# A planner that follows events, two engines that share a rate, later ranks for three pairs, and decay products ahead of the transpose

## The chip, the cores and the metric

The kernel runs on one core of a Trainium2 chip. Five engines take part: TensorE (PE: matrix products; PEld is its loading of weights), VectorE (DVE), ScalarE (ACT), GpSimd (POOL) and SyncE (SP), which here only issues transfers. Each engine works off its own list of instructions in a fixed order and waits on semaphores where it needs another's result. The metric is the device time of one execution in microseconds; a lower one is better.

## What is computed

Three layers follow each other. The first is a linear attention with a decaying state, for 4 batches, 8 heads, 768 steps and head dimension 48:

```
for t in range(S):
    cur     = einsum('bhd,bhe->bhde', u * k[t], v[t])
    y[t]    = einsum('bhd,bhde->bhe', r[t], state + cur)
    state   = w[t][..., None] * state + einsum('bhd,bhe->bhde', k[t], v[t])
```

Its output, as 3072 tokens of 384 values, goes through two gated layers (all in float32):

```
x = (sigmoid(x @ w_gate) * (x @ w_val)) @ w_out        # 384 -> 1536 -> 384
h = x @ w_in                                           # 384 -> 2048
out = (h * tanh(softplus(h))) @ w_out2                 # 2048 -> 384
```

## The kernel before

**Stages.** The 768 steps are cut into 24 chunks of 32 steps, taken two at a time: 12 pairs. For each pair the recurrence is brought into matrix form. `fine(p)` multiplies r and k within blocks of 1, 2 and 4 steps into tiles pt (L515, the helper `times`; GpSimd, for pair 0 also VectorE, by the tuple `SHARED`), sums them over the head dimension into the tile A (L535, VectorE), multiplies the diagonal by u (L515 on VectorE), and after each level folds decays into r, k and w in place (L515, blk). After three levels w at every eighth step holds the decay of eight steps.

`coarse(p)` turns r, k and w to head-dimension-first with VectorE's 32x32 transposes (`flip_k` L633 into KD, `flip_r` L629 into RD, `flip_w` L640 into WD), multiplies parts of RD by decays in WD (`scaled`, L652, three calls, on GpSimd or VectorE), and makes the score products on TensorE (`scores`, L669), whose result `merge` (L690) copies into X beside the turned A (L679). In `flip_w` the four decays of eight steps are turned, and then two small products (L644) make those of sixteen and of 32 steps. `keys(p)` folds the later decays into k, for which a small GpSimd product (`join`) first makes the decay of the last sixteen steps in place, turns k (L723, into KT) and lets ScalarE gather it into KK (L738). `states` and `states_apart` multiply keys and values on TensorE (L795, L841) and add them to the decayed state (`decay`, L772; L824, L852). `rows_out(p)` multiplies X with v and RD with the state (L887), splits the result into a high and a low half-precision part xs (L915, L918), and `turn` brings it to xt, token-last: for pairs 0 and 1 on TensorE (L939), later with a transposing transfer.

The first gated layer works on pairs of 256 tokens. `gate(p, i)` makes 24 groups of nine products per pair (L1011; twelve blocks f, each with a group for the gate and one for the value), three for each of three 128-deep parts, since every operand is held as a high and a low half. ScalarE applies the sigmoid (L1022), VectorE the product (L1027), and both split the result into gt (L1039, L1042). `out1` multiplies gt with the output weights (L1079). The weights come as 64-bit words and are decoded once on the core: `decode` and `decode_early` rescale on ScalarE (L275, L265), join on VectorE (L319, L414), cast the high part on ScalarE (L330, L424) and subtract it for the low part on GpSimd or VectorE (L333, L427). The second gated layer works on six blocks of 512 tokens (L1189, L1304) after the whole attention has ended.

**What sets the order.** The program first collects tasks. Each has one or several engines with a cost in microseconds, the tiles that it reads and writes, and a rank, its place in the program. `Plan.run` walks back from the end and gives every task a due time (`late`) from the costs and waits behind it; TensorE's tasks are due in the order of their ranks, so a rank that comes later means a later due time for all that leads to it. Then it deals out the tasks: for each engine the moment at which it could begin something that is ready, among what is ready there the earliest due; the engine with the earliest moment is served first. A task with two engines goes to the one that is served. The order found is then emitted, once and for all; the costs do not depend on what other engines do.

The main loop runs over pairs p and, in it, over the gate's twelve blocks f. Before block `YPOS[0]` = 4 it places the tasks of `tail1(p + 1)` (coarse, keys, the first states and rows of the next pair), before block `YPOS[1]` = 7 those of `tail2(p + 1)` and of `fine(p + 2)`, with the loads of pair p + 3 and of later values. SyncE's queue issues those loads in the planned order.

## Time and profile before

| | us |
|---|---|
| three runs | 939.11, 939.24, 943.17 |
| median | 939.24 |
| the profiled execution | 943.15 |
| its span | 941.4 |

The profile is of that one execution. The span runs from its first instruction to its last; 1.75 us of the execution lie around it. Busy times are sums of an engine's instructions. The row of an instruction or a group names the line of the kernel, the engine, the operation, the tile written and the tiles read, and shapes as partitions x elements; where a helper issues the instruction, the line is the helper's, so that L515 stands for products of several stages. Groups of the order of time can merge neighbours of one line under the shape of the first.

### The profile page before, as it was taken

What the parts mean: (1) busy time and instruction counts of PE and PEld (TensorE: products, weight loads), DVE (VectorE), ACT (ScalarE), POOL (GpSimd) and SP (SyncE); (2) the same over time, 40 slices, a digit from 0 to 9 for tenths busy, and PEclk for the clock granted to TensorE, in tenths of its full rate; (3) what the DMA queues carried; (4) which work ended last, traced back from release to release, by engine and by line L of the source; (5) the groups of instructions that cost most, each with busy time, mean ns of one, the idle gap of its engine ahead of it and who ended that gap; (6) DMA issues with size and microseconds to landing.
All of it is one profiled execution on the core that took longest, in us unless ns stands there. A gap on an engine that the chain in (4) does not pass through costs nothing.

```text
span 941.4 us, 29364 instructions
## 1 busy us (share of the span) xinstructions
PE 867.8 (92%) x12808; PEld 700.7 (74%) x12808; DVE 652.7 (69%) x1122; ACT 496.2 (53%) x1140; POOL 491.7 (52%) x543
## 2 busy tenths in 40 slices
PE   0376789999999999999999979999999999999998
PEld 0265678888888888888888866667677676776788
DVE  7999986487766768676779886675655556555541
ACT  2677876252525345252539656675555655556540
POOL 7997931556384655647462463553443434434330
PEclk9997979999999999999999999999999999999999
DMA  9164762222222322322216910010200102000000
GB/s 340 64 229 151 252 157 89 78 58 84 75 67 70 98 68 81 91 69 67 54 44 163 281 40 12 13 40 1 69 1 18 52 2 68 2 18 18 1 35 35
DMA packets 55313, 74.26 MB, mean 79 GB/s; under 512 B 19600, under 2 KB 36496, under 8 KB 55056
## 3 DMA queue, kind: packets, MB, share of 16 engines
q1 hardware_dynamic: 55184, 72.38, 25.6%
q8 instruction: 100, 1.64, 0.7%
q14 instruction: 29, 0.24, 0.1%
HBM read 58.99 MB, written 9.44 MB: 73 GB/s over the span
## 4 chain that ended last, share of the span: by engine, by line
PE 78%; DVE 10%; POOL 5%; ACT 4%; issue 2%; DMA 1%; SPq 0%; DVEq 0%; ACTq 0%; POOLq 0%
PE gv L1011 23%; PE h L1189 20%; PE o L1304 18%; PE o L1079 12%; PE yp L887 3%; POOL blk L515 2%; ACT KK L738 1%; PE kp L795 1%; POOL pt L515 1%; PE lp L669 1%; DVE RD L652 1%; DVE word_wp L319 1%; DVE wps L359 1%; DVE word_wi L319 1%; POOL wos L333 1%
## 5 line engine op out<-in xcount | busy, mean ns | idle before, releaser
L1189 PE MATMUL h<-x,wis 128*128 128x512 f16 x864 | 199.9, 379 | 0.0
L1011 PE MATMUL gv<-xt,wgs 128*128 128x256 f16 x1296 | 169.3, 277 | 12.7 <-DVE gt L1042 10.4
L1223 POOL TENSOR_TENSOR sum<-e 128x256 f32<-128x256 f32 x96 | 71.4, 743 | 190.8 <-ACT e L1200 190.8
L1079 PE MATMUL o<-gt,wos 128*128 128x256 f16 x1296 | 165.5, 274 | 3.1 <-POOL wos L333 1.6
L1011 PE MATMUL gv<-xt,wvs 128*128 128x256 f16 x1296 | 166.1, 276 | 1.7 <-ACT sig L1022 1.7
L1011 PEld LDWEIGHTS <-wgs 128*128 128x128 f16 x1296 | 126.3, 99 | 31.5 <-DVE gt L1042 10.7
L1189 PEld LDWEIGHTS <-wis 128*128 128x128 f16 x864 | 83.5, 98 | 82.9
L1079 PEld LDWEIGHTS <-wos 128*128 128x128 f16 x1296 | 126.5, 98 | 21.6 <-issue 1.9
L1011 PEld LDWEIGHTS <-wvs 128*128 128x128 f16 x1296 | 127.1, 99 | 18.7 <-issue 1.9
L515 POOL TENSOR_TENSOR blk<-blk 128x384 f32<-128x384 f32 (+1 forms) x138 | 120.8, 894 | 28.2 <-DMA blk<-rkw 21.0
L515 POOL TENSOR_TENSOR pt<-blk 128x384 f32<-128x384 f32 x93 | 105.0, 1156 | 27.6 <-DMA blk<-rkw 24.3
L1200 ACT ACTIVATE e<-h 128x512 f32<-128x512 f32 x96 | 57.5, 599 | 86.9 <-PE h L1189 85.9
L1027 DVE SCALAR_TENSOR_TENSOR gv<-gv,sig 128x512 f32<-128x512 f32 x72 | 50.6, 702 | 59.2 <-PE gv L1011 24.1
L1022 ACT ACTIVATE sig<-gv 128x512 f32<-128x512 f32 x72 | 42.1, 596 | 91.3 <-PE gv L1011 91.0
L1039 ACT CAST gt<-gv 128x512 f16<-128x512 f32 x72 | 42.1, 585 | 74.3 <-DVE gv L1027 74.2
L772 POOL TENSOR_TENSOR s<-s,WD 128x384 f32<-128x384 f32 x42 | 35.9, 864 | 75.9 <-DVE s L824 44.8
L1304 PE MATMUL o<-wps,gt 128*128 128x192 f16 x612 | 74.0, 246 | 0.0
L738 ACT COPY KK<-KT 32x192 f32<-32x192 f32 (+1 forms) x176 | 64.3, 365 | 5.4 <-DVE KT L723 2.8
L1242 DVE SCALAR_TENSOR_TENSOR gt<-e,gt 128x256 f16<-128x256 f32 x41 | 27.5, 681 | 49.6 <-ACT gt L1237 49.6
L1042 DVE TENSOR_TENSOR gt<-gv,gt 128x512 f16<-128x512 f32 x72 | 49.4, 687 | 16.9 <-ACT gt L1039 16.3
L1304 PE MATMUL o<-wps,wgs 128*128 128x192 f16 x498 | 59.4, 246 | 0.0
L1304 PE MATMUL o<-wps,wos 128*128 128x192 f16 x456 | 57.1, 246 | 0.0
(112 smaller groups left out, 1466.9 us busy)
## 6 DMA issues: line engine op xcount, KB each, us to landing
v<-vt SPq DMA_DIRECT2D x24, 480.0 KB, 4.1
blk<-rkw SPq DMA_DIRECT2D x22, 384.0 KB, 3.5
raw_wi<-wi SPq DMA_DIRECT2D x8, 768.0 KB, 5.3
raw_wp<-wo SPq DMA_DIRECT2D x8, 768.0 KB, 5.8
blk<-rkw SPq DMA_DIRECT2D x11, 512.0 KB, 4.1
raw_wg<-wg SPq DMA_DIRECT2D x6, 768.0 KB, 6.3
raw_wv<-wv SPq DMA_DIRECT2D x6, 768.0 KB, 5.0
raw_wo<-wo SPq DMA_DIRECT2D x6, 768.0 KB, 5.9
```

Of the source, the lines that this page charges most:

```text
L515: engines[e].tensor_tensor(out=pv, in0=a, in1=b, op=ALU.mult)
L738: nc.scalar.copy(out=to, in_=own)
L1011: nc.tensor.matmul(gps[p, i, o][:, h], w[:, a, kc, fs], xt[p][:, c, kc, :], start=(n == 0), stop=(n == 3 * KC - 1),)
L1022: nc.scalar.activation(out=sgs[p, i], in_=gps[p, i, 0], func=AF.Sigmoid, scale=1.0 / (SW * SX))
L1027: nc.vector.scalar_tensor_tensor(out=gps[p, i, 1], in0=gps[p, i, 1], scalar=SG / (SW * SX), in1=sgs.pop((p, i)), op0=ALU.mult, op1=ALU.mult,)
L1039: nc.scalar.copy(out=gt[p][:, 0, 2 * i : 2 * i + 2], in_=gps[p, i, 1])
L1042: nc.vector.tensor_tensor(out=gt[p][:, 1, 2 * i : 2 * i + 2], in0=gps[p, i, 1], in1=gt[p][:, 0, 2 * i : 2 * i + 2], op=ALU.subtract,)
L1079: nc.tensor.matmul(ops[p, c][:, :NT], wos[:, a, f, cs], gt[p][:, g, f, :], start=(f == 0 and n == 0), stop=(f == NF1 - 1 and n == 2),)
L1189: nc.tensor.matmul(hps[r, f], w2["wi"][:, a, kc, fs], x2[r][:, c, kc, :], start=(n == 0), stop=(n == 3 * KC - 1),)
L1200: nc.scalar.activation(out=es[r, f], in_=hps[r, f], func=AF.Mish, scale=ih)
L1223: engines[e].tensor_tensor(out=sums[0][:, n - 1], in0=a(), in1=b(), op=op)
L1304: nc.tensor.matmul(ops2[h, first], home(slots[r, i, name])[:, c, tsl], w2["wp"][:, a, w, i, :], start=(new and n == 0), stop=(n == 3 * NF2 ...
```

## The change

The planner's second half is replaced by a simulation that steps from event to event. A task that reads or writes the port shared by VectorE and GpSimd carries a mark `port`: all tasks that GpSimd may do, and VectorE's whole joins and the product with u. While both engines are at marked tasks, VectorE's proceeds at 0.42 and GpSimd's at 0.72 of its speed. The next task of an idle engine is the earliest due of its queue; of several idle engines the earliest due task goes first, to the engine with the lower cost. As before, no engine is left idle while its queue holds something ready.

`SHARED` now holds pairs 0 and 1. For the next pair 1 to 3 (`LATE` = 3) the recurrence is placed before blocks 9 and 11 instead of 4 and 7. The decay products of sixteen and 32 steps are made in w itself, before the transpose, which then turns seven columns instead of four; the keys use them, and their own join is dropped. Several costs are set anew. A second identity in float32 is built at the start. `turn_keys`, a path of the keys over TensorE, is added, but `TURNED` is 0, so that it is never called.

```diff
+FIRST = (9, 11)
+LATE = 3
-SHARED = (0,)
+SHARED = (0, 1)
+TURNED = 0
+SHARE = {"dve": 0.42, "pool": 0.72}
-W1LO = {"dve": 1.6, "pool": 1.85}
+W1LO = {"dve": 0.92, "pool": 1.65}
...
+        t.port = port or "pool" in t.cost
...
-        while len(order) < len(self.tasks):
-            picks = []
-            for e, queue in ready.items():
-                if queue:
-                    now = max(clock.get(e, 0.0), min(at for at, _ in queue))
-                    tired, late, rank, t = min(
-                        (bool(t.burst) and (now < rested or crowded(t)), t.late, t.rank, t)
-                        for at, t in queue
-                        if at <= now
-                    )
-                    picks.append((now, late, rank, e, t))
-            begin, _, _, e, t = min(picks, key=lambda x: x[:3])
...
+        while len(order) < len(self.tasks) or busy:
+            while True:
+                while coming and coming[0][0] <= now + 1e-9:
+                    t = heapq.heappop(coming)[2]
+                    for e in t.cost:
+                        queues.setdefault(e, []).append(t)
+                picks = []
+                for e in queues:
+                    if queues[e] and e not in busy:
+                        late, rank, t = best(e)
+                        picks.append((late, rank, t.cost[e], e, t))
+                if not picks:
+                    break
+                _, _, _, e, t = min(picks, key=lambda x: x[:3])
...
+            shared = all(e in busy and busy[e][1].port for e in SHARE)
+            rate = {e: SHARE[e] if shared and e in SHARE else 1.0 for e in busy}
+            step = min((busy[e][0] / rate[e] for e in busy), default=INF)
+            if coming:
+                step = min(step, coming[0][0] - now)
+            now += step
+            for e in list(busy):
+                busy[e][0] -= step * rate[e]
+                if busy[e][0] < 1e-9:
+                    finish(busy.pop(e)[1])
...
-        full = 1.15 if key[0] == "wo" else 0.95
-        add("dve", full, join, [low], [word])
+        add("dve", 0.85, join, [low], [word], port=True)
...
-                attn("dve", 1.2, times_u, ["U"], [pt])
+                attn("dve", 0.95, times_u, ["U"], [pt], port=True)
...
         def flip_w(e):
-            wd[p] = w = ap.tile([128, 7, BH], F32, tag=f"WD{p % 2}", name=f"WD{p}")
-            nc.vector.transpose(out=w[:, :4], in_=window(C * (DH + DP), 8 * DH, 4))
-            for n, o in ((4, 4), (6, 6)):
-                k = n // 2 if n == 4 else 1
-                i = 0 if n == 4 else 4
-                nc.vector.tensor_tensor(
-                    out=w[:, o : o + k],
-                    in0=w[:, i : i + 2 * k : 2],
-                    in1=w[:, i + 1 : i + 2 * k : 2],
-                    op=ALU.mult,
-                )
+            wd[p] = ap.tile([128, 7, BH], F32, tag=f"WD{p % 2}", name=f"WD{p}")
+            nc.vector.transpose(out=wd[p], in_=window(C * (DH + DP), 4 * DH, 7))
+
+        def join(e, out, a, b):
+            w = rows(p)[2]
+            times(e, w[:, out], w[:, a], w[:, b])
...
-        attn("dve", 1.3, flip_w, [W], [WD])
+        both = {"pool": 0.2, "dve": 0.15} if p in SHARED else {"pool": 0.2}
+        attn(both, 0, lambda e: join(e, slice(4, 13, 8), slice(0, 17, 16), slice(8, 25, 16)), [], [W])
+        attn(both, 0, lambda e: join(e, 20, 4, 12), [], [W])
+        attn("dve", 0.5, flip_w, [W], [WD])
...
-        attn({"dve": 1.2, "pool": 1.5}, 0, lambda e: scaled(e, 1, 1, 3, 0), [WD], [(*RD, 1)])
+        attn({"dve": 0.85, "pool": 1.45}, 0, lambda e: scaled(e, 1, 1, 3, 0), [WD], [(*RD, 1)])
...
-            right = w[:, m :: 2 * m].unsqueeze(2).to_broadcast([128, n, m, DH])
+            right = (w[:, 8::16] if m == 8 else w[:, 12:13]).unsqueeze(2).to_broadcast([128, n, m, DH])
...
-        attn("pool", 0.2, join, [], [W])
...
-                if f == YPOS[0]:
+                if f == (YPOS if p >= LATE else FIRST)[0]:
                     tail1(p + 1)
-                if f == YPOS[1]:
+                if f == (YPOS if p >= LATE else FIRST)[1]:
                     tail2(p + 1)
```

## Rows read from the trace of the kernel before

**Rows 1.** The page, busy time: engine, us, share of the span, instructions.
```profile
PE 867.8 (92%) x12808; PEld 700.7 (74%) x12808; DVE 652.7 (69%) x1122; ACT 496.2 (53%) x1140; POOL 491.7 (52%) x543
```

**Rows 2.** Stretches: length, busy us per engine, TensorE clock, DMA share, GB/s.
```profile
28.90:56.70 27.80, 12.23 (x460) 10.11 (x460) 26.16 (x34) 21.80 (x53) 27.41 (x25) 1.00 0.38 124
56.70:106.00 49.30, 38.05 (x744) 30.49 (x740) 48.02 (x70) 38.22 (x72) 44.34 (x43) 0.90 0.61 203
106.00:127.60 21.60, 15.97 (x341) 12.41 (x339) 19.08 (x31) 19.68 (x44) 15.03 (x13) 0.78 0.52 166
...
160.00:500.00 340.00, 338.93 (x6769) 300.35 (x6767) 243.87 (x445) 144.58 (x389) 199.11 (x213) 1.00 0.26 72
500.00:545.00 45.00, 43.38 (x682) 38.30 (x681) 40.52 (x57) 34.00 (x53) 17.98 (x17) 1.00 0.84 236
545.00:575.00 30.00, 24.55 (x215) 20.86 (x215) 22.92 (x31) 16.46 (x29) 13.63 (x14) 1.00 0.07 26
575.00:905.00 330.00, 330.00 (x2597) 228.73 (x2596) 198.07 (x381) 192.50 (x447) 143.93 (x188) 1.00 0.07 23
```

**Rows 3.** TensorE by line, 56.7-106: busy us, mean ns | idle before, releasers.
```profile
L1011 PE MATMUL gv<-xt,wgs 128*128 128x256 f16 x108 | 16.2, 303 | 4.0 <-ACT xs L915 2.1 <-DVE gt L1042 1.9
L1011 PE MATMUL gv<-xt,wvs 128*128 128x256 f16 x108 | 15.9, 302 | 0.0
L887 PE MATMUL yp<-v,X 64*32 64x48 f32 x128 | 3.6, 238 | 2.2 <-ACT X L690 2.2
...
L887 PE MATMUL yp<-s,RD 64*32 64x48 f32 x128 | 2.9, 245 | 2.6 <-DVE RD L652 2.6
```

**Rows 4.** Order of time, VectorE: start us, us, instruction.
```profile
68.74 7.33 DVE L652 TENSOR_TENSOR RD<-RD,WD 128x768 f32<-128x768 f32 x1
```

**Rows 5.** Line 652 on VectorE: ns min/median/max, first, last start.
```profile
L652 DVE TENSOR_TENSOR RD<-RD,WD x5: 411/882/7327, 26.3 to 485.0; 128x256 f32<-128x256 f32 x4, 128x768 f32<-128x768 f32 x1
```

**Rows 6.** The order of time on GpSimd beside it.
```profile
68.33 1.84 POOL L515 TENSOR_TENSOR pt<-blk 128x768 f32<-128x768 f32 x1
...
72.94 2.31 POOL L515 TENSOR_TENSOR blk<-blk 128x96 f32<-128x96 f32 x3
75.33 1.59 POOL L515 TENSOR_TENSOR pt<-blk 128x384 f32<-128x384 f32 x1
```

**Rows 7.** Groups by line and shape, VectorE, 0 to 106.
```profile
L515 DVE TENSOR_TENSOR blk<-blk 128x384 f32<-128x384 f32 x5 | 5.5, 1105 | 0.0
...
L644 DVE TENSOR_TENSOR WD<-WD 128x64 f32<-128x64 f32 x3 | 2.5, 824 | 0.1
...
L644 DVE TENSOR_TENSOR WD<-WD 128x32 f32<-128x32 f32 x3 | 2.3, 766 | 0.1
L515 DVE TENSOR_TENSOR pt<-blk 128x384 f32<-128x384 f32 x2 | 1.8, 954 | 0.0
```

**Rows 8.** Line 644 in the whole span: ns min/median/max.
```profile
L644 DVE TENSOR_TENSOR WD<-WD x24: 191/226/1057, 23.6 to 483.2; 128x64 f32<-128x64 f32 x12, 128x32 f32<-128x32 f32 x12
```

**Rows 9.** Groups by line and shape, VectorE, 63 to 106.
```profile
L535 DVE TENSOR_REDUCE A<-pt 128x32 f32<-128x768 f32 x4 | 3.8, 948 | 0.0
...
L319 DVE SCALAR_TENSOR_TENSOR word_wo<-word_wo,low_wo 128x768 uint32<-128x768 uint32 x2 | 2.8, 1412 | 0.0
L629 DVE STREAM_TRANSPOSE RD<-blk 128x512 f32<-128x512 f32 x2 | 2.3, 1144 | 0.0
...
L633 DVE STREAM_TRANSPOSE KD<-blk 128x1024 f32<-128x1024 f32 x1 | 2.0, 1967 | 0.0
```

**Rows 10.** Groups by line and shape, GpSimd, 0 to 106.
```profile
L515 POOL TENSOR_TENSOR blk<-blk 128x96 f32<-128x96 f32 x3 | 1.5, 497 | 0.0
```

**Rows 11.** The order of time on GpSimd at its first product.
```profile
5.71 1.76 POOL L515 TENSOR_TENSOR pt<-blk 128x384 f32<-128x384 f32 x1 [2.59 <-DMA blk<-rkw]
```

**Rows 12.** TensorE's waits, 500 to 575: total us, times, longest.
```profile
PE gv L1011 <- DVE gt L1042: 4.7, 2, 3.7
```

**Rows 13.** The order of time on ScalarE from 117.5.
```profile
117.89 5.84 ACT L738 COPY KK<-KT 32x192 f32<-32x192 f32 x16
```

More of the change, by code (lines that the diff above doesn't have):

```diff
@@ L72 @@
 class Task:
-    __slots__ = ("cost", "fn", "lat", "deps", "begin", "end", "late", "rank", "left", "burst", "words")
+    __slots__ = ("cost", "fn", "lat", "deps", "begin", "end", "late", "rank", "burst", "words", "port")
 class Plan:
@@ L86, in __init__, with add @@
         self.readers = {}
-    def add(self, eng, cost, fn, reads=(), writes=(), lat=SEM, burst=0.0, words=18):
+    def add(self, eng, cost, fn, reads=(), writes=(), lat=SEM, burst=0.0, words=18, port=False):
         t = Task()
@@ L132, in run, with schedule @@
                         t.late = edge = min(t.late, edge - t.cost[e])
-        clock = {}
-        ready = {}
-        order = []
-        rested = 0.0
+        for e, t in self.schedule(follow):
+            t.fn(e)
+    def schedule(self, follow):
+        now = rested = 0.0
         at_word = ORIGIN
+        coming, busy, queues, order = [], {}, {}, []
+        left = {t: len(t.deps) for t in self.tasks}
         def crowded(t):
@@ L146, in arrive, with finish, best @@
             at = max([d.end + d.lat for d in t.deps], default=0.0)
-            for e in t.cost:
-                ready.setdefault(e, []).append((at, t))
+            heapq.heappush(coming, (at, t.rank, t))
+        def finish(t):
+            t.end = now
+            for n in follow[t]:
+                left[n] -= 1
+                if left[n] == 0:
+                    arrive(n)
+        def best(e):
+            return min(
+                (bool(t.burst) and (now < rested or crowded(t)), t.late, t.rank, t)
+                for t in queues[e]
+            )[1:]
@@ L150, in run @@
         for t in self.tasks:
-            if t.left == 0:
+            if not t.deps:
                 arrive(t)
-        while len(order) < len(self.tasks):
-            picks = []
-            for e, queue in ready.items():
-                if queue:
-                    now = max(clock.get(e, 0.0), min(at for at, _ in queue))
-                    tired, late, rank, t = min(
-                        (bool(t.burst) and (now < rested or crowded(t)), t.late, t.rank, t)
-                        for at, t in queue
-                        if at <= now
-                    )
-                    picks.append((now, late, rank, e, t))
-            begin, _, _, e, t = min(picks, key=lambda x: x[:3])
-            for k in t.cost:
-                ready[k] = [x for x in ready[k] if x[1] is not t]
-            t.begin, t.end = begin, begin + t.cost[e]
-            if e == "pe":
-                at_word += t.words
-            if t.burst:
-                rested = t.end + t.burst
-            if e != "none":
-                clock[e] = t.end
-            order.append((begin, len(order), e, t))
-            for n in follow[t]:
-                n.left -= 1
-                if n.left == 0:
-                    arrive(n)
@@ L179, in run @@
-        for _, _, e, t in sorted(order, key=lambda x: x[:2]):
-            t.fn(e)
+        while len(order) < len(self.tasks) or busy:
[12 more added lines that the diff above has]
+                _, _, _, e, t = min(picks, key=lambda x: x[:3])
+                for k in t.cost:
+                    queues[k].remove(t)
+                t.begin = now
+                order.append((e, t))
+                if e == "pe":
+                    at_word += t.words
+                if e == "none":
+                    finish(t)
+                else:
+                    busy[e] = [t.cost[e], t]
+                if t.burst:
+                    rested = now + t.cost[e] + t.burst
+            shared = all(e in busy and busy[e][1].port for e in SHARE)
[8 more added lines that the diff above has]
+                    finish(busy.pop(e)[1])
@@ L183, in mixer_moe_kernel @@
+        return order
 @with_exitstack
```

76 lines of the change are left out of this document (55 added, 21 removed).

## The prediction

> **What bounds the kernel now.** I read the busy times first, then the same engines in stretches of the span, then TensorE's groups with what ended their waits, then the operations of the busiest engine in the worst stretch. TensorE is busy 867.8 of 941.4 us [rows 1], so 73.6 us are idle, and the change takes no matmul away and adds none that runs. The stretches [rows 2] say where the idle time lies: 28.9 us before the first attention product, 27.80 - 12.23 = 15.6 us from there to the first gate product, 49.30 - 38.05 = 11.25 us from 56.7 to 106.0, in which all 24 gate groups of pair 0 run (108 + 108 products, nine to a group [rows 3]), 21.60 - 15.97 = 5.6 us to 127.6, and 1.6 + 5.45 = 7.1 us in the two stretches from 500 to 575. From 160 to 500 and from 575 to 905 the idle time is 1.1 and 0.0. So only the prologue (to 128 us) and the passage to the second layer can move the end.
>
> Within the prologue the reader is to see VectorE: 26.16 of 27.80, then 48.02 of 49.30 us busy [rows 2]. GpSimd is nearly as full (27.41 and 44.34). ScalarE is not (21.80 and 38.22), but from 106.0 to 127.6 it is the fullest, 19.68 of 21.60. TensorE's waits from 56.7 to 106 are short and have many releasers: VectorE's gt 1.9 and RD 2.6, ScalarE's xs 2.1 and X 2.2 us [rows 3]. ScalarE has 11 us free there, so where it releases, it mostly came late itself. A queue that is full all the time makes everything behind it late; what counts is how much work VectorE has ahead of pair 1's gates.
>
> One row stands out. The scaling of RD that closes pair 1's recurrence took 7.33 us on VectorE [rows 4]; the five operations of this line on VectorE, four of them smaller, have a median of 0.88 us [rows 5]. It began at 68.74, while GpSimd ran its products without a pause: a group from 68.33 on, the last before the pause from 72.94 for 2.31 us, to 75.25, the next from 75.33 [rows 6]. VectorE's operation ended at 76.07, that is 0.82 us after the pause began, so it stood still for some 6.5 of its 7.33 us.
>
> **The parts of the change, in VectorE time ahead of pair 1's gates (up to 106 us).**
>
> 1. The blocked scaling. With other costs and another order it stands elsewhere. If it meets no such run, 6.5 us go; if it meets the same again, nothing does. I take -6.5, as the other four of the five lie near the median of 0.88, not near the worst [rows 5].
>
> 2. Decay products. Before, each pair had two small VectorE products after the transpose: 2.5 + 2.3 = 4.8 us for the three pairs up to 106 [rows 7], beside GpSimd; all 24 of them have a median of 0.226 us and a worst of 1.057 [rows 8]. They go. The transpose grows from 128 to 224 elements per partition; flips of 512 take 1.144 us and of 1024 1.967 [rows 9], so 0.82/512 x 96 = 0.15 us more each, 0.5 for three. Two small products come instead, ahead of the transpose, on GpSimd, where the old join of the keys goes: one more of about 0.5 us per pair (the 128x96 row has 0.497 [rows 10]), in an engine whose queue has products for pair 2 and 3 behind it that nobody waits for yet. That is the cover; without it, 0.5 us per pair. In pairs 0 and 1 VectorE may take them, at up to 1.06 each, four in all. So -4.3, at worst -0.1; I take -4.3, as GpSimd is listed for all pairs. The keys' update no longer waits for the transpose to be read.
>
> 3. VectorE may now take pair 1's products too. In pair 0 it took these: 5.5 us for five updates and 1.8 us for two products [rows 7]. The bounds are 0 and +7.3; GpSimd had taken all of pair 1's before, and VectorE's queue is the fuller one, but it takes what is ready whenever nothing more urgent is. I take the middle, +3.7. That GpSimd is relieved is hidden.
>
> 4. Later ranks. The recurrence of pairs 1 to 3 is put behind gate blocks 8 and 10 instead of 3 and 6, so its due times move by four or five gate blocks, while those of the weights and of pair 0's own chain stay. Pair 2's work that VectorE did before 106 us need not stand there: four reduces 3.8 (a pair has five, and those before 63 us are the first two pairs'), two flips of R 2.3, the flip of K 2.0, and the first two joins of the output weights 2.8 us [rows 9], 10.9 in sum. But neither planner leaves an engine idle that has something ready, so what is ready is still taken in the gaps. Bounds 0 and -10.9; half of it, -5.4. The SP queue has the loads of pair 2 and 3 with these steps; they hang on buffers, not on ranks, and I price them at nothing: the DMA engines are busy 0.38 and 0.61 of these stretches [rows 2].
>
> 5. The rest at nothing. New costs for joins and remainders move choices only. The second, wider identity is built while GpSimd waits 2.59 us for its first data [rows 11]; only what exceeds that gap would cost. The new key path over TensorE is switched off (TURNED is 0) and issues nothing. From 160 us on the events order the work anew under a TensorE that is never idle, with VectorE at 243.87 and GpSimd at 199.11 of 340 us [rows 2]: no gain is there, and slack covers a worse order. In the passage the longest item is 4.7 us for gt [rows 12]; between -5 and +5 I take 0.
>
> The sum on VectorE: -6.5 - 4.3 + 3.7 - 5.4 = -12.5 us; the ends are -21.7 and +7.2.
>
> How much of it reaches the end? Behind 106 us ScalarE is the bound (19.68 of 21.60 [rows 2]: 16 gathers of keys alone run for 5.84 us without a pause [rows 13]), so I count nothing there. Before it, relief can give TensorE back at most its idle time, 11.25 us, less the 2.2 us that it waited for X [rows 3], a string of ScalarE's own copies: 9.05, say 9.1 us. The 12.5 of VectorE cover that. What is late next is ScalarE. The granted clock was 0.90 and 0.78 in these two stretches and 1.00 later [rows 2], so with fewer gaps some matmuls may also run at the higher of the levels 1.2 and 2.4 GHz; I leave it out of the sum.
>
> The profiled execution took 943.15 us, 941.4 of them span. 943.15 - 9.1 = 934.0. It stands 3.91 us above the median of the three runs (939.24; the others are 939.11 and 943.17); the median moves alike, 939.24 - 9.1 = 930.1. Forecast: 930.
>
> **Rivals.**
>
> A. The hand-over improves more. Pair 0's own chain, 28.9 to 56.7, ran with VectorE 94% full, and much of that was pair 1's. If later ranks give pair 0 right of way there, half of the 15.6 us of idle time goes too: -9.1 - 7.8 = -16.9, some 922. For it: pair 1's reduces and flips lie in this stretch too. Against it: chains of small steps, which no rank shortens.
>
> B. VectorE is relieved and nobody profits. ScalarE's casts, gathers and copies have the same order as before and the stretch from 106 takes up what was gained; or the static order meets real durations as badly as before. Then some 2 us of the 9.1 stay: 937. For it: ScalarE's 19.68 of 21.60; the many releasers [rows 3]. Against it: ScalarE's 11 us free from 56.7 to 106. That the shared rates do not describe the engines, so that the plan is no truer than before, comes to the same time.
>
> C. Slower: VectorE is blocked again, more often. The change lets more operations go to VectorE in the very stretch in which GpSimd runs without pauses, and plans them at fixed shares, 0.42 and 0.72. The row of 7.33 us is a share of 0.82/7.33 = 0.11, and no share at all: the operation waited for a pause. With 7.3 us moved (part 3), two new blocks of 6.5, the old one gone, -4.3 of part 2 and nothing of part 4, as pair 1 then comes late and the gates of pair 1 wait: 7.3 + 13.0 - 6.5 - 4.3 = +9.5, some 949. It decides from 3.5 us of new blocking on (7.3 - 6.5 - 4.3 + 3.5 = 0). For it: the place, between 56.7 and 78. Against it: one such block among the five operations of its line [rows 5], and seven operations that VectorE took in pair 0 without one (means 1.105 and 0.954 [rows 7]).
>
> The Trainium skill has a rule that speaks for C, in "SBUF — State Buffer", section "Who interferes with whom": the port pair that VectorE and GpSimd share is an exclusive lock held for a whole instruction, and the loser blocks fully instead of being slowed in proportion. By that rule the planner's rates are the wrong form, and the time would be that of C. The trace agrees with the rule in the row of 7.33 us, which went on only when GpSimd paused.
>
> **How the numbers follow.** The forecast (924 to 935) 0.43, A 0.20, B 0.20, C 0.17. This kernel's measurement can tell about 0.5%, 4.7 us, from no change: faster is below 934.5, slower above 943.9. Faster: nearly all of the forecast's, A's and a little of B, 0.61; same: most of B and the forecast's upper edge, 0.22; slower: C, 0.17. The range goes to 914 (939.24 - 21.7 = 917.5, VectorE's lower end, and a little of the passage) and to 943 (VectorE's sum 4 us above zero); some 0.2 stays outside, nearly all of it C. The likeliest case alone: 924 to 935.
>
> **What would show it.** Part 1: no scaling of RD above 2 us on VectorE. Part 2: no products behind WD's transpose, which takes about 0.5 us, and two small GpSimd products per pair. Part 3: pt and blk products of a second pair on VectorE, at most seven. Part 4: the 24th gate group of pair 0 ends before 106, about 97, and pair 2's reduces lie behind it. The sum: TensorE's idle time before 160 us falls by about 9, and nothing changes from 160 to 905. Wrong would be: gate group 24 as late as before (B), pair 1's first gate waiting for xt with VectorE in a long two-input operation (C), the first gate group well before 56.7 (A), or a changed idle time from 500 to 575, which I set to zero.

## The result, and the profile after

The changed kernel took 927.41 us (median of four runs, 924.68 to 930.04), the kernel before 939.62 in the same comparison (939.11 to 943.17). The ratio is 0.9856, with a 95% interval of 0.9827 to 0.9885: faster by 12.2 us, where 9.1 were forecast. The profiled execution took 927.52 us, 925.8 of them span; the profiled one of before (943.15) lies at the top of its runs, so the two spans differ by 15.6.

TensorE's busy time on the page of the profile after is as it was [rows 1]; all the gain but 0.7 us is idle time:

```profile
PE 867.1 (94%) x12808; PEld 700.4 (76%) x12808; DVE 638.7 (69%) x1094; ACT 496.9 (54%) x1144; POOL 503.2 (54%) x557
```

The stretches of [rows 2] in the kernel after (start:end, length, then busy us of TensorE, its weight loads, VectorE, ScalarE and GpSimd, the granted clock, DMA share, GB/s):

```profile
28.90:56.70 27.80, 13.59 (x367) 10.59 (x350) 23.20 (x36) 23.65 (x56) 24.51 (x23) 1.00 0.48 169
56.70:106.00 49.30, 41.85 (x784) 34.06 (x783) 45.57 (x68) 42.00 (x75) 40.08 (x36) 0.93 0.65 220
106.00:127.60 21.60, 20.20 (x303) 17.30 (x300) 20.85 (x30) 16.58 (x39) 21.21 (x20) 1.00 0.56 170
160.00:500.00 340.00, 336.82 (x6820) 297.75 (x6826) 245.27 (x429) 150.61 (x392) 200.22 (x217) 1.00 0.27 72
500.00:545.00 45.00, 44.97 (x643) 40.12 (x633) 37.69 (x52) 34.80 (x57) 22.01 (x20) 1.00 0.82 226
545.00:575.00 30.00, 30.00 (x217) 21.04 (x216) 22.13 (x36) 22.04 (x46) 21.06 (x25) 1.00 0.03 10
```

Wider stretches, before and then after, make the account:

```profile
0.00:160.00 160.00, 97.84 (x2166) 80.62 (x2167) 139.45 (x193) 103.74 (x213) 113.98 (x108) 0.94 0.58 185
```

```profile
0.00:160.00 160.00, 107.80 (x2264) 89.71 (x2265) 138.27 (x200) 103.65 (x219) 121.60 (x117) 0.97 0.58 192
...
500.00:575.00 75.00, 74.97 (x858) 61.17 (x848) 59.82 (x87) 56.84 (x102) 43.07 (x45) 1.00 0.50 139
```

TensorE's idle time falls from 62.16 to 52.20 us up to 160 (-10.0, where -9.1 was forecast), rises from 1.07 to 3.18 from 160 to 500 (+2.1), and falls from 7.07 to 0.03 in the passage, 500 to 575 (-7.0, where zero was forecast). The sum, -14.9, and 0.7 us less busy time are the 15.6. In the passage VectorE was busy 3.6 us less (63.44 in [rows 2] against 59.82) and GpSimd 11.5 more (31.61 against 43.07). That is not an exchange of one for the other: 9.0 of GpSimd's us are sums of the second gated layer, as in the row below, which fall into the stretch only because the passage ends earlier. Of the weights' decoding (joins, casts and remainders of the word and sum tiles) VectorE did 35.0 us there in place of 45.2, and GpSimd 34.1 in place of 31.6; the rest came ahead of 500 or was shorter.

```profile
L1284 POOL TENSOR_TENSOR sum<-e 128x256 f32<-128x256 f32 x6 | 5.1, 843 | 4.3 <-ACT e L1261 4.3
```

The prediction spoke of events, so the same account is cut once more at two of them, the first gate product and the last product of the 24th gate group (columns as above), before and then after:

```profile
56.78:105.96 49.18, 37.93 (x742) 30.48 (x740) 47.90 (x70) 38.10 (x72) 44.22 (x43) 0.90 0.61 204
```

```profile
53.90:96.15 42.25, 35.33 (x672) 28.57 (x670) 39.67 (x62) 35.55 (x68) 35.09 (x33) 0.95 0.63 218
```

Between the two events TensorE's idle time falls from 11.25 to 6.92 us. Ahead of them it falls from 44.43 to 41.55, and behind them, to 160, from 6.48 to 3.73. So of the 10.0 us 4.3 lie where the prediction had its 9.1; 2.9 lie ahead and 2.8 behind, where it had nothing.

What the reader is to look for next are the signs that the prediction named. The 24th gate group begins its last product by 96.2, not 106.0 (forecast: about 97); the first gate product comes at 53.90, not 56.78. The block of [rows 4] is gone: line 677 is the scaling of RD, and its three operations on VectorE are short (name, count, ns min/median/max, first and last start, shapes); pair 1's ran on GpSimd. Line 670 is the transpose of the decay factors, predicted at about 0.5 us:

```profile
L677 DVE TENSOR_TENSOR RD<-RD,WD x3: 529/960/987, 26.3 to 477.4; 128x512 f32<-128x512 f32 x1, 128x768 f32<-128x768 f32 x1, 128x256 f32<-128x256 f32 x1
...
L670 DVE STREAM_TRANSPOSE WD<-blk x12: 368/383/402, 22.1 to 475.4; 128x224 f32<-128x224 f32 x12
```

The four reduces of pair 2 that stood ahead of the 24th group [rows 9] now follow it (order of time on VectorE: start, us, instruction), though that pair's transposes of R and K did not move behind it, nor did the first two joins of the output weights (90.39 and 94.19). Of the 10.9 us that part 4 names, the four reduces, 3.8, moved:

```profile
81.05 1.14 DVE L659 STREAM_TRANSPOSE RD<-blk 128x512 f32<-128x512 f32 x1
82.33 1.08 DVE L659 STREAM_TRANSPOSE RD<-blk 128x512 f32<-128x512 f32 x1
85.90 2.01 DVE L663 STREAM_TRANSPOSE KD<-blk 128x1024 f32<-128x1024 f32 x1
...
103.00 0.94 DVE L565 TENSOR_REDUCE A<-pt 128x32 f32<-128x768 f32 x1
...
114.40 1.80 DVE L565 TENSOR_REDUCE A<-pt 128x32 f32<-128x768 f32 x2
```

So the size came out and most signs are there. One sign of being wrong is there too: the idle time from 500 to 575 changed, which the prediction had set to zero. Whether the terms of the sum are true is another question: an equal total can have other summands.

### The profile page after: what moved, and what is told of

Same layout as the page of the kernel before. It is cut to its first block, busy times and chain, and to the rows that moved or that the text cites. A ratio compares the mean times of both kernels' runs of the same rounds, so it can differ in the third digit from the quotient of the medians.

```text
span 925.8 us, 29360 instructions
## 1 busy us (share of the span) xinstructions
PE 867.1 (94%) x12808; PEld 700.4 (76%) x12808; DVE 638.7 (69%) x1094; ACT 496.9 (54%) x1144; POOL 503.2 (54%) x557
## 4 chain that ended last, share of the span: by engine, by line
PE 83%; DVE 7%; ACT 4%; DMA 2%; POOL 2%; issue 1%; SPq 0%; DVEq 0%; ACTq 0%; POOLq 0%
PE gv L1072 27%; PE h L1250 20%; PE o L1365 18%; PE o L1140 13%; PE yp L948 3%; ACT KK L797 2%; PE kp L856 2%; ACT X L715 1%; DMA xt<-xs 1%; PE lp L694 1%; DVE KD L663 1%; DVE A L565 1%; POOL blk L545 1%; DVE RD L659 1%; DVE KT L782 1%
## 5 line engine op out<-in xcount | busy, mean ns | idle before, releaser
L1072 PE MATMUL gv<-xt,wgs 128*128 128x256 f16 x1296 | 167.2, 275 | 4.7 <-DMA xt<-xs 3.2
L545 POOL TENSOR_TENSOR blk<-blk 128x384 f32<-128x384 f32 (+4 forms) x150 | 125.7, 851 | 35.0 <-DMA blk<-rkw 18.7
L545 POOL TENSOR_TENSOR pt<-blk 128x384 f32<-128x384 f32 x93 | 106.9, 1173 | 38.1 <-DMA blk<-rkw 35.7
L1088 DVE SCALAR_TENSOR_TENSOR gv<-gv,sig 128x512 f32<-128x512 f32 x72 | 50.5, 702 | 55.0 <-PE gv L1072 27.9
L833 POOL TENSOR_TENSOR s<-s,WD 128x384 f32<-128x384 f32 x38 | 34.5, 918 | 51.5 <-DVE s L885 33.8
```

Of the source, the lines that this page charges most:

```text
L545: engines[e].tensor_tensor(out=pv, in0=a, in1=b, op=ALU.mult)
L1072: nc.tensor.matmul(gps[p, i, o][:, h], w[:, a, kc, fs], xt[p][:, c, kc, :], start=(n == 0), stop=(n == 3 * KC - 1),)
L1088: nc.vector.scalar_tensor_tensor(out=gps[p, i, 1], in0=gps[p, i, 1], scalar=SG / (SW * SX), in1=sgs.pop((p, i)), op0=ALU.mult, op1=ALU.mult,)
```

## The experiments

Each kernel was timed in three rounds beside the kernel before on the same chip; ratios are to that, with 95% intervals. The kernel before had a median of 939.3 to 942.3 us in these comparisons, so kernels are compared by their ratios. "Idle" is TensorE's, of 0 to 160, 160 to 500 and 500 to 575 us of the profiled execution. The last two columns are of the passage, 500 to 575: all that GpSimd did, and VectorE's part of the weights' decoding.

| kernel | median us | ratio | idle | GpSimd busy | VectorE decoding |
|---|---|---|---|---|---|
| before | 939.62 | 1 | 62.2, 1.1, 7.1 | 31.6 | 45.2 |
| the change | 927.41 | 0.9856 [0.9827, 0.9885] | 52.2, 3.2, 0.0 | 43.1 | 35.0 |
| before, products alone | 939.79 | 1.0001 [0.9987, 1.0014] | 63.3, 0.9, 6.2 | 32.1 | 44.2 |
| before, blocked scaling alone | 940.25 | 1.0010 [0.9997, 1.0024] | 59.1, 1.5, 6.2 | 32.2 | 43.6 |
| before, ranks alone | 934.42 | 0.9946 [0.9927, 0.9965] | 52.9, 2.9, 6.6 | 33.8 | 41.6 |
| before, planner alone | 933.31 | 0.9938 [0.9915, 0.9962] | 56.0, 1.0, 1.3 | 47.2 | 36.3 |
| change, ranks back | 929.78 | 0.9875 [0.9848, 0.9902] | 57.2, 0.8, 0.1 | 44.5 | 34.4 |
| change, products back | 931.32 | 0.9904 [0.9871, 0.9936] | 52.8, 2.5, 1.8 | 47.0 | 34.9 |
| change, one pair shared | 929.47 | 0.9873 [0.9843, 0.9902] | 53.8, 2.4, 0.0 | 44.5 | 34.3 |
| change, rates at one | 945.02 | 1.0033 [1.0013, 1.0053] | 57.9, 3.8, 5.8 | 37.9 | 44.2 |
| change, former planner | 944.59 | 1.0037 [1.0020, 1.0053] | 60.3, 2.9, 7.4 | 35.0 | 43.5 |
| former planner, one pair shared | 936.89 | 0.9947 [0.9925, 0.9969] | 59.5, 2.1, 7.0 | 36.6 | 39.3 |
| change, rates 0.46 and 0.76 | 929.48 | 0.9869 [0.9834, 0.9904] | 52.3, 3.7, 0.4 | 45.5 | 37.2 |
| change, exclusive planner | 923.18 | 0.9809 [0.9773, 0.9846] | 49.2, 2.6, 0.8 | 43.4 | 27.9 |

**Parts of the change taken back.** The former ranks in the changed kernel:

```
-FIRST = (9, 11)
+FIRST = YPOS
```

> The changed kernel with the recurrence of pairs 1 to 3 placed where it was (before gate blocks 4 and 7). Theory 1 (order on VectorE ahead of pair 1's gates makes the prologue's gain of 10 us; planner and rates make the passage's gain of 7 us): the 24th gate group of pair 0 ends at 103 to 106 instead of 96.4, the passage (500 to 575) stays without idle time, the time is 934 to 937. Rival (the gain is the planner's alone, ranks only label it): 96 to 98 for the 24th group, 926 to 930.

929.78 us (927.91 to 930.53): the rival's range, though the 24th gate group is late by 4.5 us (100.6), between the two expectations. The prologue's idle time rises by 5.0 us, 4.7 of them behind the 24th group (8.38 against 3.73 up to 160); the first gate product comes when it did (53.75 against 53.90). The stretch from 160 to 500 gives 2.4 back. The passage stays at 0.1, so its gain is not the ranks'.

The shared rates at one, so that the planner follows events but charges nothing for two engines at the port:

```
-SHARE = {"dve": 0.42, "pool": 0.72}
+SHARE = {"dve": 1.0, "pool": 1.0}
```

> The changed kernel with both shared rates at 1.0, so that the event planner knows nothing of the shared port. Theory 1: the 24th gate group stays within 2 us of 96.4, the idle time of the passage comes back to 4 to 7 us, the time is 931 to 935. Rival (rates matter in the prologue, where both engines are full): the 24th group ends 3 to 8 us later, 931 to 937 with a passage without idle time. Second rival (the events matter, not the rates): 926 to 929.

945.02 us (941.53 to 946.03), slower than before and above all three expectations. One line of constants carries more than the whole gain: the ratio to the change is 1.0033/0.9856 = 1.018. The profiled spans differ by 15.0 us, of which 5.7 of idle time lie ahead of 160, 0.6 behind, 5.7 in the passage, and 3.0 are busy time.

Where the first 5.7 begin is to be seen in the order of time on VectorE, from 28 us on. Line 545 is a product (pt, blk) of the recurrence, line 979 is xs, the hand-over of pair 0 to TensorE. The kernel with rates at one:

```profile
28.43 1.84 DVE L545 TENSOR_TENSOR pt<-blk 128x384 f32<-128x384 f32 x1
...
31.97 0.56 DVE L545 TENSOR_TENSOR blk<-blk 128x384 f32<-128x384 f32 x1 [1.11 <-POOL pt L545]
32.44 1.75 DVE L545 TENSOR_TENSOR pt<-pt,U 128x768 f32<-128x768 f32 x1
34.12 2.61 DVE L545 TENSOR_TENSOR pt<-blk 128x384 f32<-128x384 f32 x2
36.65 0.94 DVE L565 TENSOR_REDUCE A<-pt 128x32 f32<-128x768 f32 x1
37.51 0.77 DVE L545 TENSOR_TENSOR blk<-blk 128x384 f32<-128x384 f32 x1
38.20 0.94 DVE L565 TENSOR_REDUCE A<-pt 128x32 f32<-128x768 f32 x1
39.06 0.61 DVE L979 SCALAR_TENSOR_TENSOR xs<-yp,xs 128x192 f16<-128x192 f32 x2
```

The changed kernel in the same stretch:

```profile
34.74 0.56 DVE L545 TENSOR_TENSOR blk<-blk 128x384 f32<-128x384 f32 x1 [2.79 <-POOL blk L545]
35.22 1.75 DVE L545 TENSOR_TENSOR pt<-pt,U 128x768 f32<-128x768 f32 x1
37.07 0.62 DVE L979 SCALAR_TENSOR_TENSOR xs<-yp,xs 128x192 f16<-128x192 f32 x2
```

What TensorE waits for there, with rates at one and then in the changed kernel:

```profile
39.72 0.80 PE L1000 MATMUL xp<-first,xs 128*128 128x128 f16 x6 [7.15 <-DVE xs L979]
```

```profile
37.74 0.80 PE L1000 MATMUL xp<-first,xs 128*128 128x128 f16 x6 [3.11 <-DVE xs L979]
```

Without rates VectorE takes pair 1's products from GpSimd ahead of pair 0's hand-over (eight of line 545's pt and blk from 28 to 43 us, 9.0 us of its time, against two and 1.0 us in the change; five against one ahead of the hand-over). Some are long beside GpSimd's products: 1.84 us at 28.43, where the same shape took 0.56 at 31.97. With rates VectorE waits 2.79 us for GpSimd instead, and the hand-over comes 2 us earlier. That would make it the sharing of part 3 that goes wrong, where the planner does not charge for it; the runs on sharing below test that.

The former list planner under the other parts:

```
-        for e, t in self.schedule(follow):
-            t.fn(e)
+        (the former list scheduling)
```

> The changed kernel with the former planner (list by earliest moment, no rates); ranks, products, shared pair 1 and costs are those of the change. Theory 1: like rates of 1.0, 931 to 935, prologue kept, passage's idle time back. Rival (the planner is the whole gain): 937 to 941.

944.59 us (943.62 to 946.17), as with rates at one and above both expectations. In this kernel the event order without rates is worth nothing over the former planner; the rates are the planner's part.

The former products:

```
-        attn(both, 0, lambda e: join(e, slice(4, 13, 8), ...), [], [W])
-        attn(both, 0, lambda e: join(e, 20, 4, 12), [], [W])
-        attn("dve", 0.5, flip_w, [W], [WD])
+        attn("dve", 1.3, flip_w, [W], [WD])
```

> The changed kernel with the decay products made after the transpose on VectorE again (and the keys' join on GpSimd). Theory 1 (4.3 us of VectorE time in the first three pairs are on the path): the 24th gate group ends 2 to 4 us later, 929 to 932. Rival (these products are short and covered): 926 to 928.5.

931.32 us (930.72 to 935.51). That is the first theory's time, but not its reason: the 24th group begins its last product 0.4 us later (96.51), not 2 to 4. The prologue's idle time moves by 0.6 us and the passage's by 1.8; the order is a new one as well.

**Parts alone, put into the kernel before.** The ranks:

```
+FIRST = (9, 11)
+LATE = 3
-if f == YPOS[0]:
+if f == (YPOS if p >= LATE else FIRST)[0]:
```

> The kernel before with the later ranks of pairs 1 to 3 alone. Theory 1 of the prediction (ranks take pair 2's work out of the way): the 24th gate group ends 3 to 6 us earlier than 106, the time falls by 3 to 6 us to 935 to 938. Theory 2 (a plan is worth what its durations are; without the rates the order meets late results): the 24th group is earlier, but the time is 940 to 945, what is gained there is given back after it.

934.42 us (931.49 to 936.27): the ranks alone are worth 5 us. The expectation that they would be lost without the planner (940 to 945) fell. The prologue's idle time falls by 9.3 us, the passage keeps 6.6. But it does not fall where the first theory has it. The 24th group begins its last product at 97.49, and the first gate product comes at 48.64 instead of 56.78: ahead of it the idle time falls by 8.2 us (44.43 to 36.21), and from there to the 24th group it rises by 0.9, from 11.25 to 12.18 (columns as above):

```profile
48.64:97.49 48.85, 36.67 (x672) 29.16 (x671) 44.95 (x69) 38.99 (x74) 38.50 (x37) 0.87 0.64 209
```

That is rival A of the prediction: the later ranks give pair 0 right of way in the hand-over.

The planner, its rates, marks and new costs:

```
+SHARE = {"dve": 0.42, "pool": 0.72}
-        clock = {} ... (list scheduling)
+        for e, t in self.schedule(follow): t.fn(e)
```

> The kernel before with the event planner, its rates and marks and the new costs alone; ranks, products and shared pair as before. Theory 1: the prologue's gain is missing, the passage's is there, 933 to 936. Theory 2 (rates are the gain): most of the 13 us are there, 927 to 932, with a passage without idle time and a prologue at 55 us of idle time or less.

933.31 us (931.83 to 934.92): 6 us, the first theory's time. Here 5.8 of the passage's 7.1 us of idle time go, but the prologue's falls as well, from 62.2 to 56.0, which that theory denied. The events, the rates and the new costs are not told apart in this run. The stretch of the passage (columns as above), planner alone and then rates at one:

```profile
500.00:575.00 75.00, 73.68 (x858) 60.81 (x857) 59.72 (x83) 52.47 (x93) 47.20 (x47) 1.00 0.47 145
```

```profile
500.00:575.00 75.00, 69.23 (x837) 59.47 (x835) 61.76 (x88) 47.15 (x75) 37.92 (x34) 0.98 0.56 152
```

In every kernel that charges for the port VectorE does 28 to 37 us of the weights' decoding there, in every other 39 to 45 (table), and TensorE's idle time there is 0.0 to 1.8 us with the charge, 5.8 to 7.4 without. GpSimd's decoding does not sort the kernels so: 30 to 41 us with a charge, 30 to 38 without. No run moved the decoding alone, so that the one brings the other is argued. With rates at one, the waits are still there in TensorE's order of time:

```profile
536.64 1.33 PE L1140 MATMUL o<-gt,wos 128*128 128x256 f16 x9 [2.40 <-DVE xo L273]
...
565.92 1.16 PE L1072 MATMUL gv<-xt,wgs 128*128 128x256 f16 x9 [2.55 <-DVE gt L1103]
```

The products in the untransposed layout, at the same places of the former order:

```
+            times("pool", w[:, 4:13:8], w[:, 0:17:16], w[:, 8:25:16])
+            times("pool", w[:, 20], w[:, 4], w[:, 12])
-            for n, o in ((4, 4), (6, 6)): ... nc.vector.tensor_tensor(...)
```

> The kernel before, its plan left as it is (same tasks, costs and order); only what is issued changes: two small GpSimd products ahead of the transpose of seven columns instead of two VectorE products behind it, and no join of the keys. Prices part 2 without a new plan. Theory 1: -4.3 us on VectorE up to 106, 2 to 4 us of the time. Rival: they hang in gaps and behind GpSimd, 0 to 1 us.

939.79 us (938.35 to 941.1): nothing. VectorE is 8.9 us less busy over the span (643.8 against 652.7), and TensorE is as idle as before.

The blocked scaling of [rows 4], on the other engine at the same place of the order:

```
+            if p == 1 and to == 1:
+                e = "pool"
```

> The kernel before, its plan left as it is; the closing scaling of RD of pair 1, which took 7.33 us on VectorE, is issued on GpSimd instead. Prices part 1 without a new plan. Theory 1: VectorE is free 6.5 us earlier at 76, 3 to 6 us of the time. Rival (TensorE waited 2.6 us for it, and GpSimd comes to it only behind its run, or what follows is bound elsewhere): 0 to 2.6 us.

940.25 us (938.87 to 942.61): nothing either, though the profiled execution has 3.0 us less idle time up to 160 and its 24th group at 101.74. The scaling takes 1.49 us on GpSimd:

```profile
70.06 1.49 POOL L654 TENSOR_TENSOR RD<-RD,WD 128x768 f32<-128x768 f32 x1
```

The kernel with the products alone shows more. Its scaling stood on VectorE, in the same place of the order as the blocked one, and took 0.95 us. The reader is to see that GpSimd's next product began only at 69.49, behind a wait for a DMA; VectorE and then GpSimd:

```profile
69.20 0.95 DVE L645 TENSOR_TENSOR RD<-RD,WD 128x768 f32<-128x768 f32 x1
```

```profile
69.49 2.32 POOL L515 TENSOR_TENSOR pt<-blk 128x768 f32<-128x768 f32 x1 [0.65 <-DMA blk<-rkw]
```

In [rows 4, 6] VectorE's operation began 0.41 us after GpSimd's (68.74 and 68.33) and was blocked. Here it began 0.29 us earlier and was not; GpSimd's product took 2.32 us, not 1.84. Between these two executions of one order, the 0.65 us that GpSimd waited for a DMA went with being blocked or not.

**Sharing.** Part 3 taken back, with rates:

```
-SHARED = (0, 1)
+SHARED = (0,)
```

> The changed kernel with part 3 taken back (only the first pair's small tasks may go to either engine; planner, rates, ranks and products stay). Theory 1, the prediction's price of part 3 (sharing the second pair puts 3.7 us more on VectorE, and TensorE pays it): TensorE's idle time of the first 160 us falls from 52.2 us and the time goes to 924 to 926. Theory 2, sharing is harmless once the planner knows the shared rate, since it then puts only two block scalings of that pair on VectorE: idle 52 +-1.5, time 926 to 930. Theory 3, the choice helps (GpSimd is the engine of that pair and is full there): 929 to 934, idle of the first 160 us up by 2 or more.

929.47 us (929.3 to 930.59), idle time of the prologue 53.8, up by 1.6. Between the second and the third theory, and off the first: once it is charged for, sharing costs nothing that these runs resolve.

The same edit in the kernel with the former planner:

> The kernel with the former list planner, its ranks and products of the change, and only the first pair shared: it differs from the one of 944.6 us in the sharing alone, and from the one with the former kernel's ranks moved (934.4 us) in the costs and the products. Theory 1, a planner that does not know the shared rate is misled by the freedom to put the second pair on VectorE: 931 to 936, TensorE's idle time of the first 160 us 53 to 55 in place of 60.3, that of 500 to 575 still 6 to 7. Theory 2, the lower costs written at the two-input operations mislead a planner without rates, sharing or not: 941 to 946, idle of the first 160 us 58 or more.

936.89 us (934.11 to 942.0). By the ratio, 0.9947, it equals the ranks alone (0.9946) and is 0.9% better than with both pairs shared (1.0037), as the first theory has it. But the idle time of the prologue is the second theory's (59.5 against 60.3): of 6.4 us between the two profiled spans 4.3 are TensorE's busy time (868.0 and 863.7), since the granted clock from 56.7 to 106 was 0.91 in the one and 1.00 in the other. That sharing without rates does harm stands by the times. The place shown is the hand-over: with one pair shared no product of pair 1 stands on VectorE from 28 to 43 us and TensorE has xs at 38.04, with both pairs eight do and it has it at 39.67. The rest of the harm is not placed.

These runs also divide the 17 us of the rates. With the former planner, one pair shared in place of two gives 0.9947/1.0037, some 8 us. From there the planner with its rates gives 0.9873/0.9947, some 7 us, about what planner, rates and costs gave alone. So about half of what rates at one cost is the harm that free sharing does without them. The lower costs by themselves show no harm: with them, the new products and one pair shared, the former planner is where the ranks alone are. Rates at one with the former, higher costs were not run.

**How much is the order that a planner happens to find?** The rates moved by a little:

```
-SHARE = {"dve": 0.42, "pool": 0.72}
+SHARE = {"dve": 0.46, "pool": 0.76}
```

> The changed kernel with its two rates at 0.46 and 0.76 in place of 0.42 and 0.72: nearly the same costs, another order of the same work. It measures how much of a difference between two of these kernels is the order that a planner happens to find. Theory 1, the costs decide and the order found by chance is worth little: 925 to 930, each stretch's idle time within 1.5 us of the changed kernel's. Theory 2, chance is worth as much as the parts of the change: 931 to 940, the first 160 us off by 3 us or more.

929.48 us (927.37 to 931.23), each of the three stretches within 0.5 us of the change's idle time: here the costs decide. Inside the prologue the order is another (10.3 us idle from 56.7 to 106, 7.5 in the change), and the time is the same. Its ratio is 0.0013 above the change's. Ranks back are 0.0019 above, one pair shared 0.0017: as little, and inside the change's own interval, so neither is resolved. Products back, 0.0048 above, has an interval that overlaps the change's as well.

**The other form.** Of two operations that want the port at once, the one that began first runs on and the other stands still:

```
-            rate = {e: SHARE[e] if shared and e in SHARE else 1.0 for e in busy}
+            rate = dict.fromkeys(busy, 1.0)
+            if shared:
+                rate[max(SHARE, key=lambda k: busy[k][1].begin)] = 0.0
```

> The changed kernel with one other rule in the planner: where VectorE and GpSimd are both at an operation that takes the shared port, the one that began first goes on at its full speed and the other stands still until it ends (0.42 and 0.72 of their speeds, both at once, go out). Theory 1, what counts is that the planner charges for the two being busy at once, in whichever form: 925 to 931, TensorE's idle time of 500 to 575 under 2 us. Theory 2, the rates' form carries the gain and the exclusive form orders wrongly: 935 to 945, idle of 500 to 575 4 us or more. Theory 3, the exclusive form is the truer one, since the rows show blocked operations: under 924.

923.18 us (919.79 to 924.82), the fastest of all, and the third theory's range; the idle time of the passage, 0.8 us, is as the first has it. The two other variants of the changed kernel on the same chip, one pair shared and the moved rates, have no run below 927.37. The stretches of this kernel:

```profile
28.90:56.70 27.80, 15.13 (x368) 11.98 (x360) 27.70 (x42) 23.28 (x56) 24.38 (x23) 1.00 0.45 162
56.70:106.00 49.30, 40.05 (x787) 33.14 (x785) 47.68 (x69) 43.38 (x78) 37.20 (x33) 0.97 0.66 226
0.00:160.00 160.00, 110.77 (x2450) 94.09 (x2450) 145.99 (x215) 108.95 (x230) 116.35 (x113) 0.99 0.58 192
500.00:575.00 75.00, 74.25 (x604) 58.34 (x598) 57.25 (x87) 53.60 (x102) 43.42 (x48) 1.00 0.38 110
```

Against the change's profile, 2.8 us of idle time go (3.0 of them in the prologue) and 4.9 of busy time (862.2 against 867.1), with a granted clock of 0.99 against 0.97 up to 160; its profiled execution is the fastest of its four, so the latter is partly luck. The intervals of the two overlap (the change's begins at 0.9827, this one's ends at 0.9846), and they did not run side by side. The exclusive form is at least as good, and by the quotient of the two ratios (0.9809/0.9856) some 4 us better, which these runs do not resolve. The Trainium skill ("SBUF — State Buffer", "Who interferes with whom") says that issue order decides who blocks: the planner of this kernel is that rule. The traces agree with it, with 0.95 us for a scaling that came first (products alone) and 7.33 [rows 4] for one that came second, though that one waited for more than one instruction of GpSimd's (last section).

## Why the prediction was right, and where its working was not

The forecast of 930 and its direction held; the measured time lies in its likeliest case (924 to 935). That it came so near is in good part luck: of five parts three failed, one worked in another place than it was priced for, and the one set to zero was the largest. The parts in turn:

1. The blocked scaling, -6.5: failed. The block went, but taking the scaling off VectorE by itself gave a ratio of 0.9997 to 1.0024: 0.3 us gained at best. The row was real. Either VectorE's lost time was not on the path, or few executions have it, as the kernel with the products alone had none; the runs do not say which.
2. Decay products, -4.3: failed in the same way. The instructions went as described (transpose 0.383 us, none behind it), and alone that was worth 0.0 (0.9987 to 1.0014, -1.3 to +1.3 us). In place it is some 4 us, not set apart from the luck of another order.
3. Sharing, +3.7: failed under the rates. Two products of pair 1's went to VectorE, 1.0 us and not 3.7, and one pair shared is no faster. At rates of one it is more than the upper bound of +7.3: eight products up to 43 us, 9.0 us in all, and the hand-over's wait goes from 3.1 to 7.2 us.
4. Later ranks, -5.4: right in size as a part alone, -5.1 by the ratio (0.9946), but not in place. Alone, the gain lies in the hand-over, which part 4 did not price and rival A did; between the first gate product and the 24th group the idle time rises by 0.9 us. Within the change 5.0 us of the prologue's idle time hang on them, 4.7 of them behind the 24th group, where the sum counted nothing, and half is given back from 160 to 500, which "no gain is there, and slack covers a worse order" left out.
5. The rest at nothing: the step that failed most. In the passage "between -5 and +5 I take 0" became -7.0, and the planner's new charges, taken as moving "choices only", are worth 6 us alone (with the events and the new costs) and some 17 in place, half of which only undoes the harm of part 3. VectorE's 4.7 us of waits for gt [rows 12] were the sign: a queue with 45.2 us of decoding, some of which GpSimd could do, with GpSimd at 31.61 of 75 us.

The conversion "the 12.5 of VectorE cover that" was wrong as a method. Up to 106 us, the stretch of that sum, VectorE is busy 7.7 us less; with the rates moved it is busy only 0.9 less, and TensorE's idle time up to 160 is the same (52.3 against 52.2). With the products alone VectorE has 5.1 us less there (92.33) and TensorE idles 1.1 more. Before, the change, and the rates moved (the first busy time is TensorE's, the third VectorE's):

```profile
0.00:106.00 106.00, 50.32 (x1200) 40.65 (x1200) 97.47 (x128) 64.91 (x130) 94.95 (x92) 0.95 0.59 203
```

```profile
0.00:106.00 106.00, 57.01 (x1256) 46.21 (x1257) 89.73 (x124) 72.86 (x141) 86.24 (x84) 0.97 0.65 225
```

```profile
0.00:106.00 106.00, 56.24 (x1261) 46.02 (x1262) 96.53 (x127) 73.71 (x142) 84.72 (x83) 0.98 0.64 225
```

So what counts is not how much VectorE does but which of it stands ahead of what TensorE waits for. The cap of 9.1 was no better: it was taken from the idle time between the first gate product and the 24th group, and there 4.3 went. That ahead and behind another 5.7 went, so that 10.0 stand beside 9.1, is luck, as is that the passage's -7.0 and the +2.1 behind 160 left the total in the range.

Rival A (the hand-over improves) is there in part: TensorE's busy time of 28.9 to 56.7 went from 12.23 to 13.59, and the first gate came 2.9 us earlier. Rival B, that nobody profits, is what parts 1 and 2 do alone. Rival C did not come with the rates, but its mechanism did without them: 945 us, and the harm seen was VectorE's products ahead of the hand-over, not two more blocks of 6.5 us. C drew the wrong conclusion from a right rule: a planner with averaged rates is not the true form, yet with each of the three charges tried fewer of pair 1's products stand ahead of the hand-over on VectorE (one or two in place of five), and the time falls by 15 us or more.

Open: what part of the exclusive planner's 4 us is the clock's, what products, ranks and sharing are each worth inside the finished change, and what the rates are worth without the new costs.

## What to carry to other kernels

Value a planner's contention term by switching it off (a constant, one run) before pricing instructions: it decided 17 us here, half of them harm that another part of the change does without it, and the instructions removed decided none that could be told from nothing. Time taken off a full engine counts only if it stood ahead of something that the bounding engine was waiting for; price it by the wait that it shortens, not by the engine's busy time. Give freedom (a second engine for a task) only together with the cost that the second engine pays when both are busy.

## What the runs showed of the hardware

- One 128x768 scaling of two inputs on VectorE took 0.95 us where it began ahead of GpSimd's next product, and 7.33 [rows 4] where it began behind one and stayed blocked through a run of them.
- Who began first decided who waited, by part of an instruction. In the kernel with the exclusive planner the product with U began on VectorE 0.22 us ahead of GpSimd's product and ran its 0.94 us; GpSimd's took 1.58, where the same shape takes 0.99 (at 7.92 in the change). VectorE, then GpSimd:

```profile
33.91 0.94 DVE L547 TENSOR_TENSOR pt<-pt,U 128x768 f32<-128x768 f32 x1
```

```profile
34.13 1.58 POOL L547 TENSOR_TENSOR blk<-blk 128x384 f32<-128x384 f32 x1 [1.43 <-DVE blk L547]
```

In the change it began behind a remainder of GpSimd's and took 2.33 us; GpSimd's ended at 94.96 + 3.77 = 98.73, and 97.21 + 2.33 - 98.73 = 0.81 us are left for its own work. VectorE, then GpSimd:

```profile
97.21 2.33 DVE L545 TENSOR_TENSOR pt<-pt,U 128x768 f32<-128x768 f32 x1
```

```profile
94.96 3.77 POOL L364 TENSOR_TENSOR wos<-word_wo,wos 128x768 f16<-128x768 f32 x2 [0.15 <-ACT wos L361]
```

- That 0.81 us is the usual case and the 7.33 us the exception. In the change's trace six products with U began beside a GpSimd instruction and took 1.19 to 2.33 us; each ended 0.81 us after that instruction. In the fourteen traces together, by the start and end of every instruction, 3264 operations of VectorE with two inputs came out over 0.1 us longer than their shortest after beginning beside one of GpSimd's that had over 0.2 us left. All but five were through by 0.1 us after that one instruction's end plus their own shortest time. Four went past it by 0.4 to 1.7 us, and the one of [rows 4] by 5.0. So the row from which the prediction drew its largest term, and its rival C, is the rarest case; why it stayed blocked no run shows.
- Runs of one program spread by 7 us, in part with the granted clock: of 19 runs of the kernel before on one chip, the four at a mean clock of 0.987 took 943.1 to 944.7 us, and the nine at 0.993 to 0.995 had a mean of 940.0 (but two at 0.989 took 939.5 and 940.0). In the prologue the clock is low: the gate products of 56.7 to 106 took 0.302 us each at 0.90 [rows 2, 3], a mean over the two levels of 1.2 and 2.4 GHz. In the kernel with the former planner and one pair shared they took 0.275 at 1.00 (columns as in [rows 3]), with longer waits between them, so the clock does not simply follow the idle time:

```profile
L1049 PE MATMUL gv<-xt,wgs 128*128 128x256 f16 x117 | 15.1, 277 | 2.6 <-DVE gt L1080 2.6
L1049 PE MATMUL gv<-xt,wvs 128*128 128x256 f16 x109 | 14.0, 274 | 5.1 <-ACT sig L1060 4.4 <-issue 0.6
```
